# A hand-written order of work: w_out loaded in two halves around batch 1's k and v, half out-projection sums as filler, and a new order in every stage

## The chip, the cores and the metric

The kernel runs on one core of one Trainium2 chip. The metric is the device time of one execution in microseconds. The kernel before took 298.38 us in the median of 13 runs, from 297.27 to 302.06.

## The reference

Efficient attention (a softmax of q over the head dimension, a softmax of k over the sequence) feeds a gated feed-forward block. 8 batches, 8 heads, 576 positions, head dimension 64; the 4608 tokens of 512 features go through w_gate and w_val (512 x 1536) and w_out (1536 x 512).

```python
def _attn_ref(q, k, v):
    q_s = np.exp(q - np.max(q, axis=-1, keepdims=True))
    q_s = q_s / (np.sum(q_s, axis=-1, keepdims=True) + 1e-09)
    k_s = np.exp(k - np.max(k, axis=2, keepdims=True))
    k_s = k_s / (np.sum(k_s, axis=2, keepdims=True) + 1e-09)
    kv = np.einsum('bhsd,bhse->bhde', k_s, v)
    return np.einsum('bhsd,bhde->bhse', q_s, kv)

def _moe_ref(x, w_gate, w_val, w_out):
    g = x @ w_gate
    silu = g * (1.0 / (1.0 + np.exp(-g)))
    return (silu * (x @ w_val) @ w_out)

x = attn_out.transpose(0, 2, 1, 3).reshape(B * S, H * D)
```

## The kernel before

**Attention, per batch b and group G of four heads.** `exp` (L124) makes eq and ek from the loaded q and k on ScalarE. `cast_v` (L133) makes the bf16 v with a column of ones. `norm_sum` (L140) and `norm_mul` (L149) divide eq by its row sums to give qs. qs is transposed either by TensorE (`tr`, L158) or by a transposing DMA (`tr_dma`, L177, tile qtd). `kv` (L186) multiplies ek by v; `kn_recip` and `kn` (L200, L206) normalise it. `x` (L229) or `x_pair` (L260) multiply kn by the transposed q and cast the result into xt, the transposed input of the feed-forward block.

**Feed-forward.** Batch 0's tokens are taken whole: step I (`First`, L300) is a gate product with its Silu, step J the value product with its multiplication into hr, twelve of each. All other tokens are taken in chunks of 448 or 512 by `Pair` (L359): a pair of 128-column blocks of w_gate and w_val in seven products instead of eight, with sums of weights (gt, by `g_sum`, L333, steps Q and T) and sums of inputs (xs0 to xs3, by `x_sum`, L342, steps X for the next chunk and Y for this one). The steps of a pair are a, b, c, d, e, f, g on TensorE, with a copy, an addition or a Silu behind each, and v, an addition and a Silu. The block that is left over is done by `Direct` (L434), steps G and U.

**Out-projection.** Batch 0 goes by `Unit` (L470): step O is a token block and a half, so `O01` is the sum over the first six blocks of hr and w_out for token block 0, and `O02` the rest, with the copy and store. Later tokens go by `Quad` (L510), again seven products instead of eight, steps A, B, C, D, E, F, H, with sums of hr (hs, `h_sum`, L494, steps S) and sums of w_out (wt, `w_sum`, L488, steps W).

**The order.** Nothing is scheduled by a tool: each plan is a string of step names, and `chunk` (L746) issues them in that order, so every engine runs its own share of the steps in the order of the string. `PLAN_B` handles batch 0's I, J and O steps beside batch 1's attention, `PLAN_0` the rest of the first 1024 tokens, `PLAN` the five middle chunks, `PLAN_N` the two chunks after the last attention, `PLAN_E` the last out-projection. A number behind a colon is a batch; without one it is two ahead of the chunk. A star changes the engine:

```python
ceng = nc.vector if alt else nc.scalar        # copies of a Pair or Quad
meng = nc.vector if alt else nc.gpsimd        # multiplications into hr
elif nm == "cv":
    cast_v(b, G, nc.vector if alt else nc.gpsimd)
elif nm == "nd":
    norm_mul(b, G, nc.gpsimd if alt else nc.vector)
```

`si` and `pe` are tiny activations that load ScalarE's Silu or Exp table early. `kk` is kv with kn for batch 1, `xz` is x for batch 1, `lo` the loads of the next batch.

**Queues.** Loads of q, k and v, transposing DMAs and stores are issued from SyncE's queue (SP), in the order of the program; w_gate, w_val and w_out from GpSimd's queue (POOL), ahead of or between GpSimd's own work. `load` takes an `after`: the issue waits for that DMA to land. q has three buffers, k and v two each. PSUM has eight banks of one tag, shared by all steps.

Of the kernel before, what the change touches and what calls it, by code (L numbers as in the profile page):

```python
# [16 lines left out]
def kernel(  # L17
# [21 lines left out]
    B, H, S, D = q.shape  # L39
# [27 lines left out]
    wo = const.tile([128, MT, d_model], FP16, name="wo", tag="wo")  # L67
# [9 lines left out]
    dmas = {}  # L77
    raw = {}

    def load(b, G, what, src, after=None):  # L80
        raw[what, b, G] = ld.tile(
            [128, 2, T * 64], FP32, tag=what, name=what, bufs=3 if what == "q" else None
        )
        ap = bass.AP(
            tensor=src.tensor,
            offset=src[b, 4 * G].offset,
            ap=[[T * 64, 128], [2 * HSTR, 2], [1, T * 64]],
        )
        d = nc.sync.dma_start(out=raw[what, b, G], in_=ap)
        if after is not None:  # L90
            tc.add_manual_dep(d.ins, after.ins.name, SYNC, reason="order of loads")
        dmas[what, b, G] = d

    def load_group(b, G):
        for what, src in (("q", q), ("k", k), ("v", v)):
            load(b, G, what, src)
# [9 lines left out]
    def wo_slice(m0, n):  # L106
        ap = bass.AP(
            tensor=moe_w_out.tensor,
            offset=moe_w_out[m0 * 128, 0].offset,
            ap=[[d_model, 128], [128 * d_model, n], [1, d_model]],  # L110
        )
        return nc.gpsimd.dma_start(out=wo[:, m0:m0 + n, :], in_=ap)
# [9 lines left out]
    A, Z = BANKS = ((0, 5), (5, 9))  # L122
# [10 lines left out]
    def cast_v(b, G, eng, t0=0, t1=T):  # L133
        copy(
            eng,
            vbs[G][:, t0:t1, 0:128].rearrange("p t (h d) -> p t h d", d=64),
            raw["v", b, G].rearrange("p h (t d) -> p t h d", d=64)[:, t0:t1],
        )
# [38 lines left out]
    def tr_dma(b, G):  # L177
        s = st[b, G]
        qt = at.tile([128, T, 2, 64], BF16, tag="qtd", name="qtd")
        nc.sync.dma_start_transpose(  # L180
            out=qt.rearrange("p t g c -> p t (g c)"),
            in_=s["qs"].rearrange("p t c -> p (t c)"),
        )
        s["qt"] = [qt[:, :, g, :] for g in range(2)]
# [417 lines left out]
    with tc.manual_schedule():  # L602
# [22 lines left out]
        w_dma = []  # L625
# [6 lines left out]
        tc.add_manual_dep(w_dma[0].ins, dmas["k", 0, 0].ins.name, SYNC, reason="order of loads")  # L632
        load(1, 0, "q", q, after=w_dma[4])
        load(1, 1, "q", q)
        for m0 in (0, 4, 8):
            w_dma.append(wo_slice(m0, 4))
        tc.add_manual_dep(w_dma[7].ins, w_dma[5].ins.name, SYNC, reason="order of loads")

        warm_up(WARM[0])
# [18 lines left out]
        x(0, 1, A)  # L658
        x(0, 1, Z)

        load(1, 0, "k", k, after=w_dma[8])
        load(1, 0, "v", v)
        load(1, 1, "k", k, after=w_dma[9])
        load(1, 1, "v", v)
        load(2, 0, "q", q, after=dmas["k", 1, 0])
        load(2, 0, "k", k, after=dmas["v", 1, 0])
        load(2, 0, "v", v, after=dmas["k", 1, 1])
        load(2, 1, "q", q, after=dmas["v", 1, 1])
        load(2, 1, "k", k, after=dmas["q", 2, 0])

        n_ch = n_tok // 512 - 1

        def op(t, ci, c0, h, parts):
            alt = t.endswith("*")
            t = t.rstrip("*")
            t, b = t.split(":") if ":" in t else (t, ci + 2)
            b = int(b)
            k, a, nm = t[0], t[1:], t[:2]
            if nm in ATT:
                G = int(t[2]) if t[2:3].isdigit() else 0  # L680
                if b >= B or nm == "lo" and b + 1 >= B and ci >= 0:
                    return
                if nm == "eq":
                    exp(b, G, "q")
                elif nm == "ek":
                    exp(b, G, "k")
                elif nm in ("si", "pe"):
                    f = AF.Silu if nm == "si" else AF.Exp
                    nc.scalar.activation(out=warm, in_=zero[:, 0:1], func=f)
                elif nm == "cv":  # L690
                    cast_v(b, G, nc.vector if alt else nc.gpsimd)
                elif nm == "ns":
                    norm_sum(b, G)
                elif nm == "nm":
                    norm_mul(b, G, nc.vector if alt else nc.gpsimd)
                    tr_dma(b, G)
                elif nm == "lo":
                    if ci < 0:
                        load(b, 1, "v", v)
                    else:  # L700
                        load_group(b + 1, 0)
                        load_group(b + 1, 1)
                elif nm == "kv":
                    kv_pair(b)
                elif nm == "xx":
                    x_pair(b, nc.scalar if alt else nc.vector)
                elif nm == "nd":
                    norm_mul(b, G, nc.gpsimd if alt else nc.vector)
                elif nm == "tr":
                    tr(1, G, BANKS[int(t[3])], nc.vector)  # L710
                elif nm == "kk":
                    kv_kn(b, G, split=True)
                elif nm == "xz":
                    x(1, G, BANKS[int(t[3])], nc.scalar if alt else nc.vector)
            elif k in "abcdefgv":
                parts["p" + a].run(k, alt)
            elif k in "GU":
                parts["m" + a].run(k)
            elif k in "IJ":
                parts["i" + a].run(k)  # L720
            elif k == "O":
                parts["u" + a[0]].run(int(a[1]), alt)
            elif k in "ABCDEFH":
                parts["o"].run(k, alt)
            elif k in "SR":
                k0 = int(a[1])
                h_sum(ci + (k == "R"), int(a[0]), k0, k0 + int(a[2]))
            elif k == "X":
                if ci + 1 < n_ch:
                    x_sum(c0 + 2 * h, 256, int(a), nc.gpsimd if alt else nc.vector)  # L730
            elif k == "Y":
                x_sum(c0, h, int(a), nc.gpsimd if alt else nc.vector)
            elif k == "W":
                w_sum(int(a), nc.gpsimd if alt else nc.vector)
            elif k == "Q":
                g_sum(int(a), nc.vector if alt else nc.gpsimd)
            elif k == "T" and ci == B - 2:
                i = int(a)
                if i == 0:
                    parts["t"] = ld.tile(  # L740
                        [128, 4, 2, 2, 128 * (HM - NP)], FP16, tag="q", name="gt2", bufs=3
                    )
                gt2[i] = parts["t"][:, i]
                g_sum(i, nc.gpsimd if alt else nc.vector, 128 * NP, 128 * HM, gt2)
# [11 lines left out]
            for t in plan.split():  # L756
                op(t, ci, c0, n // 2, parts)

        ATT = ("pe", "eq", "ek", "si", "cv", "ns", "nm", "lo", "kv", "xx", "nd", "tr", "kk", "xz")
        ORDER = (0, 1, 2, 3, 4, 5)  # L760
        gt2 = [None] * 4
        PLAN_B = """
        I0 I1 pe:1 I2 I3 J0 J1 I4 I5 J2 J3 J4 Q0 I6 J5 I7 J6 J7 eq0:1 ns0:1 eq1:1 I8
        nd0:1* ns1:1 J8 I9 J9 I10 Q1* nd1:1* I11 cv0:1 tr00 J10 J11 tr10 ek0:1 O01 Q3*
        cv1:1 ek1:1 O11 tr01 kk0:1 O02 tr11 eq0:2 O12 kk1:1 ns0:2 O21 xz10* ek0:2 xz00*
        O22 Q2 xz01 eq1:2 cv0:2 xz11 O31 load:2 nm0:2 cv1:2 O32 ek1:2
"""
        PLAN_0 = """
        a0 ns1 G5 b0 G11 Y0 c0 Y2 Y1 v0 Y3* d0* W2 a1 f0 b1 U5 c1 g0 d1 W0 v1 e0 a2 f1 b2
        v2 kv silu:2 nm1 g1 d2 a3 e1 c2 f2 b3 c3 e2 g2 d3 v3 e3 a4 f3 xx* load g3 W1 d4*  # L770
        b4 c4* X0 f4 v4 U11 e4* X2* X1 W3 X3 g4*
"""
        PLAN = """
        a0 S042 b0 G5 c0 d0 A v0 S002 a1 f0 b1 S142 c1 v1 U5 S242 g0 pe S222 B S022 S102
        S122 S302 d1 S322 ek0 e0 a2 S342 e1 eq0 ns0 S202 C ek1 f1 D E eq1 cv1 b2 c2* silu
        F nm0 cv0 g1 d2 v2 ns1 a3 nm1 H* f2 kv g2 d3 b3 c3 v3 e2 load f3 e3 a4 b4 c4 g3 v4
        d4* e4 xx* f4 X2 G11 g4 X0 X1 X3* U11
"""
        PLAN_N = """
        a0 S222 b0 c0 d0 T0* A v0 S002 f0 a1 e0* S042 b1 g0 d1 c1 S022 v1 a2 f1 S242 S102  # L780
        b2 e1* c2 g1 S142 d2 v2 B f2 a3 T1* b3 c3 S342 S122 S202 g2* e2 d3 C S302 v3 f3
        e3* S322 a4 b4 g3* d4 c4 v4 D T2 f4 e4* a5 b5 g4* c5* X0* d5 F f5 v5 E T3* X1 e5*
        X3 g5* H* X2*
"""
        PLAN_E = """
        S022 A S042 S122 S002 S142 S202 B C S102 S302 S322 S242 S222 S342 D E F H*
"""
        chunk(-1, 0, S, PLAN_B)
        chunk(0, S, 1024 - S, PLAN_0)
        for ci in range(1, n_ch):  # L790
            chunk(ci, 512 * (ci + 1), 512, PLAN if ci + 2 < B else PLAN_N)
# [31 lines left out]
```

The softmax here doesn't subtract the row's maximum and nothing guards it: scores larger than these inputs give would overflow.

## Time and profile before

| | |
|---|---|
| Median of 13 runs | 298.38 us (297.27 to 302.06) |
| The profiled execution's own time | 297.96 us, span 296.1 us |
| TensorE (PE) busy | 286.2 us, 2716 matmuls |
| VectorE (DVE) busy | 240.9 us |
| ScalarE (ACT) busy | 221.4 us |
| GpSimd (POOL) busy | 156.1 us |
| TensorE clock granted | 1.00 throughout |
| Read from HBM, written | 37.75 MB, 9.44 MB |

| Stage, us from the span's start | length | PE busy | DVE | ACT | POOL |
|---|---|---|---|---|---|
| 15.70 to 36.30, batch 0's I and J steps | 20.60 | 19.91 | 10.20 | 15.45 | 7.85 |
| 36.30 to 55.90, rest of PLAN_B | 19.60 | 18.30 | 16.28 | 11.89 | 13.33 |
| 55.90 to 76.30, PLAN_0 | 20.40 | 19.09 | 16.92 | 15.90 | 14.71 |
| 106.30 to 136.25, a middle chunk | 29.95 | 29.95 | 26.40 | 25.34 | 19.27 |
| 253.70 to 281.20, a late chunk | 27.50 | 27.50 | 22.69 | 19.00 | 3.99 |

Times in the views are in microseconds from the first instruction unless they are marked ns. A row of the timeline gives the start, the length, the engine, the line and operation, the tiles and shapes and how many instructions were merged; square brackets hold the idle time ahead of it and what ended it. A row of the waits gives who waited for whom, the total, how often and the longest. A row of the groups gives the busy total and the mean of one in ns, then the idle time before. The matmuls of PE are pipelined, so that a record is longer (0.27 for 256 columns) than the interval from one start to the next (0.109).

### The profile page before, as it was taken

What the parts mean: (1) busy time and instruction counts of PE and PEld (TensorE: products, weight loads), DVE (VectorE), ACT (ScalarE), POOL (GpSimd) and SP (SyncE); (2) the same over time, 40 slices, a digit from 0 to 9 for tenths busy, and PEclk for the clock granted to TensorE, in tenths of its full rate; (3) what the DMA queues carried; (4) which work ended last, traced back from release to release, by engine and by line L of the source; (5) the groups of instructions that cost most, each with busy time, mean ns of one, the idle gap of its engine ahead of it and who ended that gap; (6) DMA issues with size and microseconds to landing.
All of it is one profiled execution on the core that took longest, in us unless ns stands there. A gap on an engine that the chain in (4) does not pass through costs nothing.

```text
span 296.1 us, 7118 instructions
## 1 busy us (share of the span) xinstructions
PE 286.2 (97%) x2716; PEld 233.8 (79%) x2716; DVE 240.9 (81%) x490; ACT 221.4 (75%) x416; POOL 156.1 (53%) x128
## 2 busy tenths in 40 slices
PE   8999998998999999999999999999999999999992
PEld 6877664587888878887888688868887888888882
DVE  2935696797999889988898889888999898897881
ACT  5684955877799689968996889688969775778431
POOL 1903856679329852975197619761977444031000
PEclk9999999999999999999999999999999999999999
DMA  7999999928903793199326961795192000500065
GB/s 261 292 192 245 243 320 380 269 62 161 359 2 72 151 355 129 23 188 348 147 51 138 295 224 39 152 321 193 30 152 45 0 2 1 125 19 2 9 136 143
DMA packets 38338, 46.47 MB, mean 157 GB/s; under 512 B 16288, under 2 KB 21408, under 8 KB 38304
## 3 DMA queue, kind: packets, MB, share of 16 engines
q1 hardware_dynamic: 32864, 41.03, 48.4%
q0 software_dynamic: 5280, 4.72, 10.0%
q8 instruction: 21, 0.34, 0.5%
q10 hardware_dynamic: 160, 0.26, 0.2%
q14 instruction: 13, 0.11, 0.1%
HBM read 37.75 MB, written 9.44 MB: 159 GB/s over the span
## 4 chain that ended last, share of the span: by engine, by line
PE 74%; DMA 15%; POOL 3%; ACT 3%; DVE 2%; issue 1%; ACTq 0%; SPq 0%; DVEq 0%; POOLq 0%
PE sx L388 23%; PE ox L533 13%; PE sw L388 11%; PE ow L533 7%; PE sy L388 6%; DMA wg<-in_moe_w_gate_dram 4%; DMA q<-in_q_dram 4%; PE oy L533 4%; DMA wo<-in_moe_w_out_dram 3%; PE u_ps L441 3%; PE g_ps L441 3%; PE kv L192 2%; DMA qtd<-qs 2%; POOL qs L152 1%; PE o_ps L479 1%; DMA k<-in_k_dram 1%
## 5 line engine op out<-in xcount | busy, mean ns | idle before, releaser
L388 PEld LDWEIGHTS <-gt 128*128 128x128 f16 x672 | 64.6, 98 | 13.5 <-issue 3.0
L432 POOL TENSOR_TENSOR hr<-sg,u 128x512 bf16<-128x512 f16 (+1 forms) x33 | 39.1, 1184 | 51.5 <-ACT sg L431 50.5
L388 PE MATMUL sx<-xs,gt 128*128 128x256 f16 (+1 forms) x336 | 49.9, 271 | 0.3 <-DVE s L118 0.3
L116 ACT COPY s<-sx 128x512 f32<-128x512 f32 (+1 forms) x77 | 44.3, 577 | 7.7 <-PE sx L388 7.4
L423 POOL TENSOR_TENSOR hr<-sg,u 128x512 bf16<-128x512 f16 (+1 forms) x31 | 36.5, 1185 | 23.1 <-DVE u L422 22.3
L533 PEld LDWEIGHTS <-hs 128*128 128x128 bf16 x384 | 37.2, 98 | 4.7
L152 POOL TENSOR_TENSOR qs<-eq,rr 128x1152 bf16<-128x1152 bf16 x15 | 32.6, 2179 | 9.2 <-DVE rr L147 6.0
L388 PEld LDWEIGHTS <-wg 128*128 128x128 f16 x336 | 32.8, 98 | 4.8
L427 DVE TENSOR_TENSOR u<-sx,s 128x512 f16<-128x512 f32 (+1 forms) x42 | 28.5, 679 | 9.8 <-ACT sg L414 4.0
L414 ACT ACTIVATE sg<-s 128x512 f16<-128x512 f32 (+1 forms) x42 | 26.2, 625 | 12.8 <-DVE s L412 11.0
L431 ACT ACTIVATE sg<-sx 128x512 f16<-128x512 f32 (+1 forms) x42 | 25.2, 601 | 10.7 <-PE sx L388 10.6
L533 PEld LDWEIGHTS <-hr 128*128 128x128 bf16 x288 | 28.2, 98 | 3.3
L412 DVE TENSOR_TENSOR s<-sy,s 128x512 f32<-128x512 f32 (+1 forms) x42 | 28.3, 675 | 2.7 <-PE sy L388 2.1
L422 DVE TENSOR_TENSOR u<-sw,s 128x512 f16<-128x512 f32 (+1 forms) x42 | 28.4, 675 | 2.5 <-PE sw L388 1.2
L143 DVE TENSOR_REDUCE rs<-eq 128x18 f32<-128x1152 bf16 x16 | 21.4, 1340 | 7.0 <-ACT eq L127 7.0
L388 PE MATMUL sx<-xt,gt 128*128 128x256 f16 (+1 forms) x168 | 25.0, 271 | 0.0
L388 PE MATMUL sw<-xs,wv 128*128 128x256 f16 (+1 forms) x168 | 25.0, 271 | 0.0
L388 PE MATMUL sy<-xt,wg 128*128 128x256 f16 (+1 forms) x168 | 25.0, 271 | 0.0
L388 PE MATMUL sw<-xs,gt 128*128 128x256 f16 (+1 forms) x168 | 24.9, 271 | 0.0
L388 PE MATMUL sx<-xt,wg 128*128 128x256 f16 (+1 forms) x168 | 24.9, 271 | 0.0
L116 ACT COPY s<-sw 128x512 f32<-128x512 f32 (+1 forms) x34 | 19.8, 582 | 5.4 <-PE sw L388 5.2
L533 PE MATMUL ox<-wt,hs 128*128 128x256 f16 x192 | 23.6, 273 | 0.0
(101 smaller groups left out, 552.4 us busy)
## 6 DMA issues: line engine op xcount, KB each, us to landing
q<-in_q_dram SPq DMA_DIRECT2D x16, 576.0 KB, 6.5
k<-in_k_dram SPq DMA_DIRECT2D x16, 576.0 KB, 6.5
v<-in_v_dram SPq DMA_DIRECT2D x16, 576.0 KB, 7.1
out_dram<-o_sb SPq DMA_DIRECT2D x70, 128.0 KB, 2.4
wv<-in_moe_w_val_dram POOLq DMA_DIRECT2D x3, 512.0 KB, 11.2
wo<-in_moe_w_out_dram POOLq DMA_DIRECT2D x3, 512.0 KB, 10.1
wg<-in_moe_w_gate_dram POOLq DMA_DIRECT2D x2, 512.0 KB, 11.2
wg<-in_moe_w_gate_dram POOLq DMA_DIRECT2D x2, 256.0 KB, 5.0
```

The source lines that it names most:

```text
L116: nc.scalar.copy(out=out, in_=in_)
L143: nc.vector.reduce_sum(out=rs, in_=s["eq"].rearrange("p t h d -> p (t h) d"), axis=mybir.AxisListType.X)
L152: eng.tensor_mul(s["qs"].rearrange("p t (h d) -> p (t h) d", d=64), s["eq"].rearrange("p t h d -> p (t h) d"), s["rr"].to_broadcast([128, ...
L388: nc.tensor.matmul(out=bank[:, h * j:h * j + h], lhsT=wgt(kk, j), rhs=rhs[:, kk, 0:h], start=first and j == 0 and kk == 0, stop=kk == 1, s ...
L412: nc.vector.tensor_add(self.s1, self.y[:, 0:w], self.s1)
L414: nc.scalar.activation(out=self.sa[:, 0:w], in_=self.s1, func=AF.Silu)
L422: nc.vector.tensor_add(u, self.w[:, 0:w], self.s2)
L423: meng.tensor_mul(self.out(0), self.halves(self.sa), self.halves(u))
L427: nc.vector.tensor_add(self.u, self.x[:, 0:w], self.s5)
L431: nc.scalar.activation(out=sb[:, 0:w], in_=self.x[:, 0:w], func=AF.Silu)
L432: meng.tensor_mul(self.out(1), self.halves(sb), self.halves(self.u))
L533: nc.tensor.matmul(out=dst[p][:, 0:HN], lhsT=lhs(kk, p), rhs=rhs(kk), start=start and i == 0, stop=i == HM - 1, skip_group_check=True,)
```

## The change

w_out is loaded in four slices of three blocks instead of three slices of four. The first two stand where the slices stood. The other two (`wo`) are issued from the plan, on GpSimd's queue, after J11. Batch 1's k and v of group 0 no longer wait for w_out but for batch 1's q; k of group 1 waits for the second slice. The load of v for batch 2's group 1 has a step of its own (`lv`). PLAN_B is merged into PLAN_0, in a new order with other engines for some steps, and the other plans have new orders too, with the stars placed anew.

```diff
--- before.py
+++ after.py
@@ -632,8 +632,8 @@
         tc.add_manual_dep(w_dma[0].ins, dmas["k", 0, 0].ins.name, SYNC, reason="order of loads")
         load(1, 0, "q", q, after=w_dma[4])
         load(1, 1, "q", q)
-        for m0 in (0, 4, 8):
-            w_dma.append(wo_slice(m0, 4))
+        for m0 in (0, 3):
+            w_dma.append(wo_slice(m0, 3))
         tc.add_manual_dep(w_dma[7].ins, w_dma[5].ins.name, SYNC, reason="order of loads")
 
         warm_up(WARM[0])
@@ -658,15 +658,15 @@
         x(0, 1, A)
         x(0, 1, Z)
 
-        load(1, 0, "k", k, after=w_dma[8])
+        load(1, 0, "k", k, after=dmas["q", 1, 1])
         load(1, 0, "v", v)
-        load(1, 1, "k", k, after=w_dma[9])
-        load(1, 1, "v", v)
-        load(2, 0, "q", q, after=dmas["k", 1, 0])
-        load(2, 0, "k", k, after=dmas["v", 1, 0])
-        load(2, 0, "v", v, after=dmas["k", 1, 1])
-        load(2, 1, "q", q, after=dmas["v", 1, 1])
-        load(2, 1, "k", k, after=dmas["q", 2, 0])
+        load(1, 1, "k", k, after=w_dma[8])
+        load(1, 1, "v", v, after=dmas["k", 1, 0])
+        load(2, 0, "q", q, after=dmas["k", 1, 1])
+        load(2, 0, "k", k, after=dmas["v", 1, 1])
+        load(2, 0, "v", v, after=dmas["q", 2, 0])
+        load(2, 1, "q", q, after=dmas["k", 2, 0])
+        load(2, 1, "k", k, after=dmas["v", 2, 0])
 
         n_ch = n_tok // 512 - 1
 
@@ -678,7 +678,7 @@
             k, a, nm = t[0], t[1:], t[:2]
             if nm in ATT:
                 G = int(t[2]) if t[2:3].isdigit() else 0
-                if b >= B or nm == "lo" and b + 1 >= B and ci >= 0:
+                if b >= B or nm == "lo" and b + 1 >= B:
                     return
                 if nm == "eq":
                     exp(b, G, "q")
@@ -694,12 +694,14 @@
                 elif nm == "nm":
                     norm_mul(b, G, nc.vector if alt else nc.gpsimd)
                     tr_dma(b, G)
+                elif nm == "lv":
+                    load(2, 1, "v", v)
+                elif nm == "wo":
+                    wo_slice(6, 3)
+                    wo_slice(9, 3)
                 elif nm == "lo":
-                    if ci < 0:
-                        load(b, 1, "v", v)
-                    else:
-                        load_group(b + 1, 0)
-                        load_group(b + 1, 1)
+                    load_group(b + 1, 0)
+                    load_group(b + 1, 1)
                 elif nm == "kv":
                     kv_pair(b)
                 elif nm == "xx":
@@ -756,36 +758,33 @@
             for t in plan.split():
                 op(t, ci, c0, n // 2, parts)
 
-        ATT = ("pe", "eq", "ek", "si", "cv", "ns", "nm", "lo", "kv", "xx", "nd", "tr", "kk", "xz")
+        ATT = ("pe", "eq", "ek", "si", "cv", "ns", "nm", "lo", "kv", "xx", "nd", "tr", "kk", "xz", "lv", "wo")
         ORDER = (0, 1, 2, 3, 4, 5)
         gt2 = [None] * 4
-        PLAN_B = """
-        I0 I1 pe:1 I2 I3 J0 J1 I4 I5 J2 J3 J4 Q0 I6 J5 I7 J6 J7 eq0:1 ns0:1 eq1:1 I8
-        nd0:1* ns1:1 J8 I9 J9 I10 Q1* nd1:1* I11 cv0:1 tr00 J10 J11 tr10 ek0:1 O01 Q3*
-        cv1:1 ek1:1 O11 tr01 kk0:1 O02 tr11 eq0:2 O12 kk1:1 ns0:2 O21 xz10* ek0:2 xz00*
-        O22 Q2 xz01 eq1:2 cv0:2 xz11 O31 load:2 nm0:2 cv1:2 O32 ek1:2
-"""
         PLAN_0 = """
-        a0 ns1 G5 b0 G11 Y0 c0 Y2 Y1 v0 Y3* d0* W2 a1 f0 b1 U5 c1 g0 d1 W0 v1 e0 a2 f1 b2
-        v2 kv silu:2 nm1 g1 d2 a3 e1 c2 f2 b3 c3 e2 g2 d3 v3 e3 a4 f3 xx* load g3 W1 d4*
-        b4 c4* X0 f4 v4 U11 e4* X2* X1 W3 X3 g4*
+        I0 I1 I2 I3 J0 J1 J2 I4 I5 J3 I6 J4 I7 I8 J5 pe:1 J6 eq0:1 J7 J8 eq1:1 I9 I10
+        ns0:1 ns1:1 J9 I11 Q2 J10 ek0:1 nd1:1 nd0:1* O01 tr00 tr01 tr10 tr11 cv0:1 kk0:1
+        ek1:1 Q0* O11 cv1:1* xz00* xz01* O21 kk1:1 J11 wo xz10* Q1 eq0:2 lv xz11 O31 a0 b0
+        Y0* ek0:2 O02 ns0:2 c0 O12 W0 Y1 Y2 cv1:2 d0 nm0:2 O22 Y3 eq1:2 ek1:2 Q3* W1 f0 v0
+        a1* b1 cv0:2 e0 g0 G5 d1* c1 ns1:2 v1 nm1:2 a2 f1 O32 kv:2 g1 d2 b2 c2 v2 e1 f2 a3
+        G11 e2* b3 g2 v3 U5 d3* xx:2* load:2 c3* f3 W2* a4* silu:2 b4 c4 g3 v4 d4* U11 X0*
+        f4 e3* e4* X2 X1 W3 g4* X3
 """
         PLAN = """
-        a0 S042 b0 G5 c0 d0 A v0 S002 a1 f0 b1 S142 c1 v1 U5 S242 g0 pe S222 B S022 S102
-        S122 S302 d1 S322 ek0 e0 a2 S342 e1 eq0 ns0 S202 C ek1 f1 D E eq1 cv1 b2 c2* silu
-        F nm0 cv0 g1 d2 v2 ns1 a3 nm1 H* f2 kv g2 d3 b3 c3 v3 e2 load f3 e3 a4 b4 c4 g3 v4
-        d4* e4 xx* f4 X2 G11 g4 X0 X1 X3* U11
+        S002 pe a0 b0 c0 A d0 S042 S242 S142 S022 B eq0 S102 eq1 S122 G5 v0 f0 e0 S202 a1
+        b1 D v1 c1* S222 S322 g0* S302 a2* d1 C S342 e1 cv0 cv1 f1 ek0 F E ek1 g1 d2 b2 H*
+        c2 ns1 v2 a3 nm1 ns0 f2 b3 nm0 kv g2 d3 c3 v3 a4 f3 b4 e2* e3 c4 g3 d4 v4 e4 G11
+        f4 xx X2 load X0 X1 U5 X3 g4* silu U11
 """
         PLAN_N = """
-        a0 S222 b0 c0 d0 T0* A v0 S002 f0 a1 e0* S042 b1 g0 d1 c1 S022 v1 a2 f1 S242 S102
-        b2 e1* c2 g1 S142 d2 v2 B f2 a3 T1* b3 c3 S342 S122 S202 g2* e2 d3 C S302 v3 f3
-        e3* S322 a4 b4 g3* d4 c4 v4 D T2 f4 e4* a5 b5 g4* c5* X0* d5 F f5 v5 E T3* X1 e5*
-        X3 g5* H* X2*
+        S002 a0 b0 c0 d0 A v0 S042 S022 f0 B a1 S142 S102 g0* b1 d1 c1 S242 v1 a2 S222
+        S122 e0 f1 b2 S202 S302 D g1 d2 c2 v2 e1* a3 f2 S322 e2 b3 c3 g2 v3 d3* C f3 T0 a4
+        b4 v4 T1* e3* g3 T2* d4 S342 c4 F f4 a5 b5 T3* g4 d5* e4 c5 v5 f5 E e5* g5* X0 X1
+        H* X2 X3
 """
         PLAN_E = """
-        S022 A S042 S122 S002 S142 S202 B C S102 S302 S322 S242 S222 S342 D E F H*
+        S022 S042 S002 S142 S122 S342 A S102 S242 S222 S202 S322 B S302 C D* E F H*
 """
-        chunk(-1, 0, S, PLAN_B)
         chunk(0, S, 1024 - S, PLAN_0)
         for ci in range(1, n_ch):
             chunk(ci, 512 * (ci + 1), 512, PLAN if ci + 2 < B else PLAN_N)
```

## The prediction

> **What bounds the kernel now.** I read the page's busy shares first. PE is busy 97%, but the Trainium skill (Perfetto Trace Analysis, section Identifying the Most-Contended Engine) warns that matmul busy time of a pipelined engine says little of headroom, so I checked it against the work. In the chain of waits the kv matmuls of the middle chunks start at 96.28, 126.25, 156.22, 186.18 and 216.15, a period of 29.97. The matmuls of a chunk, at the start-to-start intervals in the trace, are 224 of 256 columns x 0.109 = 24.4, 16 of 512 x 0.216 = 3.5, kv 1.2 and the x matmuls 0.85: 29.9. So the middle is full, and nothing can be won there. Next the waits of PE, with the rows of its timeline:
>
> ```profile
> PE 286.2 (97%) x2716; PEld 233.8 (79%) x2716; DVE 240.9 (81%) x490; ACT 221.4 (75%) x416; POOL 156.1 (53%) x128
> ```
> ```profile
> PE kv L192 <- POOL vb L118: 1.1, 2, 0.7
> PE xa L273 <- DMA qtd<-qs: 0.9, 1, 0.9
> PE g_ps L310 <- ACT sg L321: 0.7, 1, 0.7
> ```
> ```profile
> 36.33 2.26 PE L310 MATMUL g_ps<-xt,wg 128*128 128x320 f16 x16 [0.72 <-ACT sg L321]
> ...
> 44.65 0.70 PE L192 MATMUL kv<-vb,ek 64*128 64x129 bf16 x18 [0.73 <-POOL vb L118]
> ...
> 48.62 0.70 PE L192 MATMUL kv<-vb,ek 64*128 64x129 bf16 x18 [0.35 <-POOL vb L118]
> ...
> 51.16 0.46 PE L237 MATMUL xp<-qt,kn 64*64 64x320 bf16 x6 [0.19 <-ACT kn L212]
> ...
> 59.82 0.54 PE L388 MATMUL sx<-xs,gt 128*128 128x224 f16 x4 [0.33 <-DVE s L118]
> ...
> 72.45 0.33 PE L273 MATMUL xa<-qtd,kn 64*64 64x320 bf16 x4 [0.94 <-DMA qtd<-qs]
> ```
> All avoidable waits lie between 35 and 76 us. Counted from start to start, less the nominal interval (a wait costs a drained pipeline too), they are 0.89, 0.89, 0.51, 0.51, 0.50 and 1.21, with two small ones 0.20 and 0.17: **4.9 us**, the most that a new order can win before the tail. Why kv is late stands in the chain:
>
> ```profile
> 27.31 10.12 DMA wo<-in_moe_w_out_dram
> ...
> 37.48 4.01 DMA k<-in_k_dram
> ...
> 41.50 7.30 DMA q<-in_q_dram
> ```
> Batch 1's k leaves only when the second third of w_out has landed (37.42), so exp, the cast of v and kv follow the transfer.
>
> **What the skill says.** GPSIMD Engine Reference, Specifications: GpSimd shares its SBUF interfaces with VectorE, and they contend when a VectorE instruction has two SBUF inputs. The trace agrees: an h_sum of VectorE (L502) takes 0.416 alone and up to 1.36 when a GpSimd run is under way; gt at 37.91 took 2.78 and ended 0.69 after GpSimd's qs, where its twin took 0.81. It works both ways: the cast of v at 60.19 took 1.45 instead of 1.14. DMA: Bandwidth & Descriptors, Queues, rings and completion order: a DMA engine round-robins between queues by packet. The trace agrees: q of batch 1 (SP queue) and the last w_val slice (POOL queue) finish together, at 30.8 and 30.5.
>
> **The change, part by part.** The orders on each engine come from building both kernels, the durations from the profile. PE has the same 2716 matmuls.
>
> *Batch 0, 15.7 to 38.4.* 23 I and J steps of 0.98 from 15.72 end at 38.4. exp(q) of batch 1 ends when q lands (33.35) + 1.2 = 34.55, plus a table load 1.28 and Silu 0.75 frees I9's banks at 36.6. Before, I10 came 20 steps in (35.4) and waited for Silu behind those exps; now the first step that wants these banks is J10 at 37.4. The 0.89 goes.
>
> *DMAs.* Two w_out slices of three blocks are 1.5 x 2.55 = 3.8 instead of 2 x 2.55 us of transfer ahead of k(1,1); k(1,0) and v(1,0) leave at 33.4 instead of 37.5. With 1.5 a load, k(1,0) lands at about 37.3 (was 41.5), v(1,0) 38.9 (43.3), k(1,1) 40.3, v(1,1) 41.8 (47.3). The other two slices are issued on GpSimd behind the cast of v(1,0), at about 40 (2 x 0.76, hidden: the next GpSimd work waits for VectorE's gt at 44). They share the engines with q and k of batch 2. Each later load waits for the one two ahead, so v(2,1) lands at about 55, between 52.4 (3.5 from issue to landing, nothing in its way) and 57.
>
> *38.4 to 55.* O01 (1.29) and tr00, tr01 end at 40.2. tr10 needs qs of group 1, now on VectorE: it is free at 39.3, but the cast of v(1,0) holds the port to 40.05, and the multiply needs 1.2: 41.2, **a stall of 0.9** (0.3 to 1.3). exp(k) is done at 40.8: kv runs at once. Then out-projection halves fill. The next kv waits for the cast of v(1,1), moved to VectorE behind gt (2 x 0.8) from 43.3: about 1.3 for 1152 elements (640 took 0.77), to 46.1; PE is there at 45.5: **0.6**. x of group 1 waits for J11's multiply in one bank: **0.4**. The wo halves land long before O02 at 50.8.
>
> *55 to 75.* VectorE runs seven two-input sums in a row (W0, Y1 to Y3, two gt, W1), 51.3 to 55.8; f0's addition comes behind them and g0 wants it at 57.1. GpSimd then waits for v(2,1): cast, qs (2.1), cast, to 60.4, just ahead of kv at 60.8. Small waits there and at g1: **0.4**. The second qtd leaves GpSimd at about 64.7 and takes 4.5 as at 67.74: 69.2 against x at 68.8: **0.4** (was 1.21). End: 0.1. Sum 2.8 against 4.9: **2.1 won**. I take 0.5 off for a landing of v(2,1) inside that run (below).
>
> *Middle chunks.* VectorE takes three multiplies (0.425), three casts of x (1.6) and X3 (0.42): +3.3; it loses port waits, (0.62-0.42) and (0.59-0.42) x 3 in L502 and L506 and 0.5 in X2: -1.6. 26.4 + 1.7 = 28.1 of 29.95. GpSimd loses 4.7. ScalarE loses 1.5 of casts, but exp is split in two places with Silu between: two more table loads of 1.28; 25.4 + 1.0 = 26.4. Walking a chunk from a0, the deadlines that come nearest: d0 (2.6) needs a0's copy behind a table load (2.2); f2 (18.3) needs d2's copy behind g1's reload (17.5 to 18.2); g2 (20.4) needs f2's addition (20.1); the second qtd lands at 25.5 to 26.3, x at 27. All hold, none by much. I take **0.1 lost in all**, 0 to 0.3 a chunk as bounds. c0 of chunk 1 waits for X0 on GpSimd, behind W2 (about 3.1, scaled from 2.61 for 1280 columns): ready at 75.1, wanted at 75.8.
>
> *Last chunks and tail.* Seven multiplies and two copies of VectorE instead of eight and one, A later in VectorE's order but at the same place on PE: no change. The tail after the last matmul keeps its order: 0.
>
> Sum: 297.96 (the profiled execution: span 296.1 and 1.9 around it) - 2.1 + 0.5 + 0.1 = 296.5; that execution lies 0.4 under the median 298.38, so **296.8**.
>
> **Rivals.**
> (1) *The gain is given back in the start-up, no change.* The casts and qs on GpSimd come later than I walk (v(1,0) after 39.4, v(2,1) after 57): tr10, kv(2) and qtd lose 1 to 2 us more. For it: the loads' landings are estimates. Against: they are issued 4 us earlier. About 298.3.
> (2) *GpSimd takes the port inside VectorE's run, slower.* If v(2,1) lands before about 53.3, GpSimd's cast, qs and cast (1.15 + 2.1 + 1.15) can slip between the seven sums, since a waiting engine seems to be served when an instruction ends (the h_sum at 90.54 got in between two GpSimd runs). The last sum ends 60, g0 waits 3.6 instead of 0, later waits of 0.8 vanish: net 2.8 more lost, 299.6. For it: the lower bound 52.4. Against: the w_out slices in the way.
> (3) *ScalarE becomes the bound in the middle, slower.* If the reloads make copies late by 0.5 in five chunks: 2.5, 299.3. For it: margins of 0.1 to 0.4. Against: back-to-back ScalarE records overlap by 0.1 each, which I did not credit.
> (4) *Everything holds*, including the port: up to 4 won, 294.6.
>
> **How the numbers follow.** Forecast 0.48 (own range 295.6 to 297.4), rival 4 0.06, rival 1 0.2, rivals 2 and 3 0.13 each. 0.3% of 298.4 is 0.9 us, about what a measurement of this kernel can tell from no change. Faster: forecast and rival 4, less a little of the forecast's upper end, 0.52; same 0.21; slower 0.27. Range 295.0 to 299.8: outside lie most of rival 4 and the bad ends of 2 and 3.
>
> **What would show it.** Right: no wait of g_ps for sg near 35; kv of batch 1 at about 41.8 (was 44.65); a wait of tp or kv of some 0.9 near 40.5 and one of kv for VectorE's cast near 45.5; the first sx of chunk 1 near 75 (was 76.48); the kv period still 29.97. Wrong: g0 waiting over 2 us near 57 behind the sums (rival 2), a period over 30.2 (rival 3), or kv of batch 1 at 44 (rival 1).

## The result: slower, and the profile after

The changed kernel takes **302.91 us** in the median of 11 runs, from 301.72 to 309.01, against 298.38 us: a ratio of **1.0139** (95% interval 1.0117 to 1.0161), some 4.2 us more. Ratios, here and below, leave out executions that lie over 1.5% above the fastest of their kernel (10 of 22 in the run e11); medians do not. The profiled execution took 302.49 us, with a span of 300.3.

First the page's busy shares after the change:

```profile
PE 288.0 (96%) x2716; PEld 235.3 (78%) x2716; DVE 243.0 (81%) x530; ACT 221.9 (74%) x401; POOL 135.4 (45%) x112
```

As many matmuls, in a span 4.2 us longer, with 1.8 us more of busy time: matmuls must have become slower somewhere too. The waits of PE (total, times, longest) and the rows of its timeline that answer to those of before:

```profile
PE kv L192 <- POOL vb L118: 3.2, 2, 2.9
PE kv L192 <- DVE vb L118: 2.2, 1, 2.2
```
```profile
41.25 0.70 PE L192 MATMUL kv<-vb,ek 64*128 64x129 bf16 x18 [0.32 <-POOL vb L118]
...
47.31 0.70 PE L192 MATMUL kv<-vb,ek 64*128 64x129 bf16 x18 [2.19 <-DVE vb L118]
...
65.28 1.22 PE L192 MATMUL kv<-vb,ek 64*128 64x129 bf16 x36 [2.92 <-POOL vb L118]
66.44 0.92 PE L388 MATMUL sx<-xt,gt 128*128 128x224 f16 x4
67.15 0.95 PE L388 MATMUL sx<-xs,gt 128*128 128x224 f16 x4
...
70.03 0.55 PE L388 MATMUL sx<-xs,gt 128*128 128x224 f16 x4
```

kv of batch 1 starts 3.4 us earlier than before (44.65), and no g_ps waits for sg near 35 any more. But kv now stands still twice for a cast of v. And behind the second pause a row of four matmuls of 224 columns takes 0.95 instead of 0.55. The windows (PE, PEld, DVE, ACT and POOL busy, then the granted clock, the DMA share and GB/s) give that stretch a number:

```profile
62.00:66.00 4.00, 1.08 (x28) 0.81 (x27) 1.14 (x3) 3.02 (x7) 4.00 (x4) 1.00 0.14 28
66.00:70.00 4.00, 4.00 (x38) 3.27 (x33) 2.15 (x9) 1.44 (x3) 4.00 (x4) 0.57 0.56 111
```

The chain of waits (start, length) has lost the w_out transfer that stood in it before. It now goes from batch 1's v over the casts and gt:

```profile
33.20 6.07 DMA v<-in_v_dram
...
39.40 1.80 POOL vb L118
...
42.56 1.56 DVE gt L340 x2
44.12 3.15 DVE vb L118
47.27 0.04 issue
47.31 0.70 PE kv L192 x18
...
64.14 1.10 POOL vb L118
65.24 0.04 issue
65.28 0.74 PE kv L192 x19
```

Who makes the casts late stands in the timelines of VectorE and GpSimd:

```profile
42.56 1.56 DVE L340 TENSOR_TENSOR gt<-wv,wg 128x1280 f16<-128x1280 f16 x2
44.03 3.22 DVE L118 CAST vb<-v 128x1152 bf16<-128x1152 f32 x1
```
```profile
43.47 6.11 POOL L340 TENSOR_TENSOR gt<-wv,gt 128x1280 f16<-128x1280 f16 x2 [0.76 <-DVE gt L340]
...
60.92 1.14 POOL L118 CAST vb<-v 128x1152 bf16<-128x1152 f32 x1 [8.78 <-DMA v<-in_v_dram]
62.03 2.12 POOL L152 TENSOR_TENSOR qs<-eq,rr 128x1152 bf16<-128x1152 bf16 x1
64.09 1.14 POOL L118 CAST vb<-v 128x1152 bf16<-128x1152 f32 x1
```

VectorE's cast of v(1,1) takes 3.22 us and ends 0.7 after GpSimd's first gt sum (the row of 6.11 holds two, the first from 43.47 to 46.57). GpSimd stands idle for 8.78 us until v(2,1) has landed at 60.8, and the cast of v(2,0), whose data had been there since 52.8, comes only behind that cast and a multiply: kv starts at 65.28.

Start-to-start, by stage:

| | before | after | difference |
|---|---|---|---|
| to the first I step | 15.72 | 15.28 | -0.44 |
| from there to the first sx of chunk 1 | 60.76 | 64.83 | +4.07 |
| chunks 1 to 7 | 204.98 | 205.92 | +0.94 |
| last out-projection to its last matmul's end | 9.36 | 9.41 | +0.05 |
| from there to the end | 5.29 | 4.85 | -0.44 |

The 0.94 is 0.26 and 0.24 in chunks 1 and 3, 0.23 and 0.28 in the two late chunks; the other middle chunks are within 0.03 of 29.97.

### The profile page after: what moved, and what is told of

The parts are those of the page before. It is cut to its first block, busy times and chain, and to the rows that moved or that the text cites. A ratio compares the mean times of both kernels' runs of the same rounds, so it can differ in the third digit from the quotient of the medians.

```text
span 300.3 us, 7094 instructions
## 1 busy us (share of the span) xinstructions
PE 288.0 (96%) x2716; PEld 235.3 (78%) x2716; DVE 243.0 (81%) x530; ACT 221.9 (74%) x401; POOL 135.4 (45%) x112
## 4 chain that ended last, share of the span: by engine, by line
PE 82%; DMA 7%; DVE 4%; POOL 3%; ACT 1%; issue 1%; ACTq 0%; SPq 0%; DVEq 0%; POOLq 0%
PE sx L388 23%; PE ox L533 12%; PE sw L388 11%; PE ow L533 7%; PE sy L388 6%; PE warm_ps L256 4%; PE u_ps L441 4%; PE oy L533 3%; PE g_ps L441 3%; PE kv L192 3%; DMA q<-in_q_dram 3%; DMA v<-in_v_dram 2%; PE g_ps L310 2%; POOL qs L152 2%; PE o_ps L479 2%; DMA qtd<-qs 2%
## 5 line engine op out<-in xcount | busy, mean ns | idle before, releaser
L423 POOL TENSOR_TENSOR hr<-sg,u 128x512 bf16<-128x512 f16 (+1 forms) x28 | 32.1, 1147 | 100.2 <-DVE u L422 47.1
L388 PEld LDWEIGHTS <-gt 128*128 128x128 f16 x672 | 65.5, 98 | 14.2 <-issue 1.5
L116 ACT COPY s<-sx 128x512 f32<-128x512 f32 (+1 forms) x70 | 40.7, 582 | 8.3 <-PE sx L388 8.0
L431 ACT ACTIVATE sg<-sx 128x512 f16<-128x512 f32 (+1 forms) x42 | 24.7, 589 | 16.7 <-PE sx L388 11.5
L432 POOL TENSOR_TENSOR hr<-sg,u 128x512 bf16<-128x512 f16 (+1 forms) x27 | 30.7, 1138 | 14.0 <-ACT sg L431 14.0
L152 POOL TENSOR_TENSOR qs<-eq,rr 128x1152 bf16<-128x1152 bf16 x14 | 29.5, 2120 | 6.0 <-DVE rr L147 6.0
L116 ACT COPY s<-sw 128x512 f32<-128x512 f32 (+1 forms) x36 | 21.4, 594 | 9.6 <-PE sw L388 9.6
L388 PE MATMUL sw<-xs,wv 128*128 128x256 f16 (+1 forms) x168 | 24.2, 273 | 0.0
```

Source lines behind the costliest of these rows:

```text
L116: nc.scalar.copy(out=out, in_=in_)
L152: eng.tensor_mul(s["qs"].rearrange("p t (h d) -> p (t h) d", d=64), s["eq"].rearrange("p t h d -> p (t h) d"), s["rr"].to_broadcast([128, ...
L388: nc.tensor.matmul(out=bank[:, h * j:h * j + h], lhsT=wgt(kk, j), rhs=rhs[:, kk, 0:h], start=first and j == 0 and kk == 0, stop=kk == 1, s ...
L423: meng.tensor_mul(self.out(0), self.halves(self.sa), self.halves(u))
L431: nc.scalar.activation(out=sb[:, 0:w], in_=self.x[:, 0:w], func=AF.Silu)
L432: meng.tensor_mul(self.out(1), self.halves(sb), self.halves(self.u))
```

## Experiments

**One cast at a time.** Theory T: the two late casts and the slow stretch behind the second are the loss; R1: the later orders are; R2: the held cast is most of it.

```diff
- Q0* O11 cv1:1* xz00* xz01* O21 kk1:1 J11 wo xz10*      # e1
+ Q0* O11 wo cv1:1 xz00* xz01* O21 kk1:1 J11 xz10*
- a1* b1 cv0:2 e0                                        # e2; e4 has both
+ a1* b1 cv0:2* e0
```

> The cast of v(1,1) goes from VectorE back to GpSimd, ahead of its gt sum; the two w_out slices are issued ahead of it, so that they leave as before. Theory T (two late casts of v, the second set by the landing of v(2,1) at 60.8 and by GpSimd's order behind it, then a slow stretch of TensorE): the cast ends at about 44.8, kv(1,1) at 45 does not wait and the 2.2 us there are gone, but TensorE now reaches kv of batch 2 at about 60.0 instead of 62.3, and the cast it waits for still ends near 65.2: its wait grows from 2.9 to some 5.2, and the total stays at 302.5 to 302.9. Rival R2 (VectorE's held cast is the main loss by itself): the gain of 2.3 stays, 300.6. Rival R1 (the loss lies in the new orders of the later chunks): no change, and no growth of the wait at kv of batch 2.

Measured 302.81 us, ratio 1.014 (1.0078 to 1.0201): no change, as T has it. But the 2.2 us went elsewhere than expected. The waits of PE:

```profile
PE o_ps L479 <- DMA wo<-in_moe_w_out_dram: 2.5, 1, 2.5
PE kv L192 <- POOL vb L118: 2.4, 2, 2.1
```

TensorE, 2 us earlier, runs into the fourth w_out slice (landed at 53.7); kv of batch 2 still starts at 65.56, when v(2,1)'s cast and what stands behind it are done. R2's 300.6 lies just outside the wide interval of these four executions, and e4 below repeats the finding with 18. R2 falls: the held cast is hidden by transfers that come later.

> The cast of v(2,0) goes from GpSimd, where it stands behind the cast of v(2,1) and a 2.1 us multiply, to VectorE at the same place of the order. T: VectorE does it near 59.5 to 61 in about 1.3 us, GpSimd being idle there; v(2,1)'s cast ends at 62.1 as before, TensorE comes to kv of batch 2 at 62.3 and does not wait; without the pause TensorE's matmuls behind it run at full rate: 3.1 + 1.65 = 4.7 us less, 298.2. If the slow stretch is not due to the pause, 299.8. R1 (later orders): at most 1 us less, 302. If GpSimd's multiply holds VectorE's cast (3 us instead of 1.3): 299.5 to 300.

Measured 300.92 us, 1.0071 (1.0047 to 1.0094): 2.0 us won, not 4.7. In the profiled execution the slow stretch is gone (clock 1.000). VectorE's timeline gives the cast without GpSimd beside it:

```profile
59.34 0.81 DVE L118 CAST vb<-v 128x1152 bf16<-128x1152 f32 x1
```

0.81 us, where the same cast took 3.22. What took the place of the stall, in PE's timeline:

```profile
64.46 1.20 PE L192 MATMUL kv<-vb,ek 64*128 64x129 bf16 x35 [1.20 <-ACT sg L431]
...
73.72 0.33 PE L273 MATMUL xa<-qtd,kn 64*64 64x320 bf16 x4 [1.48 <-ACT xt L116]
```

ScalarE's exp of k(2,1) waits until that load lands at 60.84; the table load and the Silus stand behind it in order, and kv's second bank waits for one of them.

> Both edits: v(1,1) cast on GpSimd, v(2,0) cast on VectorE. T: TensorE reaches kv of batch 2 at about 60.0, v(2,1) still lands near 60.8 and its cast ends at 62.1: a wait of about 2.1, which only replaces the one removed at 45; total as with v(2,0)'s cast moved alone, 298.0 (299.6 if a pause of 2.1 us is enough for a slow stretch). R2: the gains add, 295.8.

Measured 300.87 us, 1.0079 (1.0055 to 1.0103): as e2 alone, so the gains do not add. R2 is out again. T has the size of the wait (2.1), but neither its last releaser, since kv now waits 1.88 for ScalarE, behind k(2,1), nor the time of 298.0.

**Where the landing comes from.** In the kernel before, each load waits for one four loads ahead (q(2,0) for k(1,0), k(2,1) for q(2,0)); in the changed one mostly for one two ahead. T2: with two loads under way the engines run dry. R3: w_out beside the loads lowers the rate. Rows of SyncE's queue in the changed kernel (q, k, v of group 0, then of group 1):

```profile
40.77 0.37 SPq L89 DMA_DIRECT2D q<-in_q_dram  x1
43.62 0.37 SPq L89 DMA_DIRECT2D k<-in_k_dram  x1
47.02 0.37 SPq L89 DMA_DIRECT2D v<-in_v_dram  x1
51.52 0.37 SPq L89 DMA_DIRECT2D q<-in_q_dram  x1
52.83 0.37 SPq L89 DMA_DIRECT2D k<-in_k_dram  x1
53.24 0.47 SPq L89 DMA_DIRECT2D v<-in_v_dram  x1
```

Between 47.4 and 51.5 nothing is issued: the queue waits for k(2,0) to land (51.51).

```diff
- load(2, 0, "v", v, after=dmas["q", 2, 0])
- load(2, 1, "q", q, after=dmas["k", 2, 0])
- load(2, 1, "k", k, after=dmas["v", 2, 0])
+ load(2, 0, "v", v)
+ load(2, 1, "q", q, after=dmas["q", 2, 0])
+ load(2, 1, "k", k)
```

With both cast edits:

> Both cast edits, and three waits between loads loosened: v(2,0) is issued without a wait, q(2,1) waits for q(2,0) instead of k(2,0), k(2,1) for nothing. Order of instructions unchanged. Theory T2 (what is left is the landing of k(2,1) and v(2,1), late because SyncE's queue stands still until k(2,0) has landed, and ScalarE's exp of k(2,1) holds the Silus behind it): q, k and v of group 1 leave near 46 instead of 52.5, v(2,1) lands near 58.5 instead of 61 to 63, ScalarE is free of exp at 60.2, kv of batch 2 waits 0.3 instead of 2.1, x of batch 2 does not wait (1.5 before): 3.2 us less than with both casts alone, 297.6. Rival R3 (the transfers themselves are the limit, w_out and the loads of batch 2 share the engines at a lower rate): v(2,1) lands where it did, within 1 us: 300.5 to 301.

Measured 299.07 us, 1.0025 (0.9997 to 1.0054). v(2,1) landed at 58.0, as T2 has it; R3's 300.5 lies outside. The profiled execution took 297.98 us, 0.4 above T2's 297.6: VectorE's cast met GpSimd again, and PE waited 1.0 for the copy behind it. The median is 1.1 higher still, which this profile does not explain. VectorE's row, then GpSimd's:

```profile
58.35 1.64 DVE L118 CAST vb<-v 128x1152 bf16<-128x1152 f32 x1
```
```profile
59.27 2.57 POOL L152 TENSOR_TENSOR qs<-eq,rr 128x1152 bf16<-128x1152 bf16 x1
```

Then the loads alone, in the changed kernel:

> The changed kernel with the three waits between loads loosened and nothing else; both casts stay where the change put them. T2 (v(2,1) lands late because SyncE's queue stands still until k(2,0) has landed; GpSimd's order and the slow stretch follow from that): v(2,1) lands near 58, GpSimd's cast, multiply and cast end at 62.4, TensorE is at kv of batch 2 at 62.3: a wait of 0.1 to 0.3 instead of 2.9, no slow stretch there, 4.5 us less: 298.3. The 2.2 us for VectorE's cast at 45 stay. R3 (rate of transfer): 302 to 302.9.

Measured 299.49 us, 1.0032 (1.0011 to 1.0052): 3.4 us won by three waits, short of the 4.5 expected. In the profiled execution (300.81 us, 1.3 above the median) v(2,1) landed at 59.3, issued at 50.0, since q(2,0) landed late there; kv of batch 2 did not wait, but the slow stretch had come behind the first pause, and x of batch 2 waited 1.3 for the second qtd. One window of the kernel before, two of the changed kernel, then two of the kernel with casts and loads:

```profile
46.00:50.00 4.00, 3.65 (x36) 1.96 (x35) 1.85 (x9) 2.52 (x4) 2.58 (x2) 1.00 1.06 391
```
```profile
50.00:54.00 4.00, 4.00 (x26) 2.42 (x25) 3.90 (x9) 3.05 (x5) 1.03 (x1) 1.00 0.70 199
...
58.00:62.00 4.00, 4.00 (x34) 2.92 (x31) 3.58 (x7) 3.12 (x4) 1.07 (x1) 1.00 0.46 167
```
```profile
50.00:54.00 4.00, 3.57 (x25) 2.14 (x23) 3.90 (x7) 2.20 (x4) 2.29 (x2) 1.00 1.05 403
...
58.00:62.00 4.00, 2.98 (x25) 2.21 (x24) 4.00 (x5) 3.97 (x6) 3.83 (x3) 1.00 0.03 11
```

The DMA share is 1.06 in the kernel before. From 50 to 54 it is 0.70 in the changed kernel and 1.05 in the one with casts and loads, which is done with them at 58.

**The title's edit undone, and its loads alone.**

```diff
- for m0 in (0, 3):                                      # e12, with `wo` out of the plan
+ for m0 in (0, 3, 6, 9):
```

> The title's edit undone in the changed kernel: all four w_out slices are issued where the three stood, none from the plan. T2 and R3 both: batch 1's k and v share the engines with w_out and land about 2 us later, kv of batch 1 at 43 instead of 41.25. R3 (the two late slices slow the loads of batch 2): those now run undisturbed, v(2,1) lands by 56.5 although the waits stay, no wait at kv of batch 2: 299 to 300. T2 (the waits alone): v(2,1) still lands after 59 and the pause ahead of kv of batch 2 stays at 2 or more: 302 to 304.

Measured 302.53 us, 1.0137 (1.0097 to 1.0177): no better. With w_out out of the way the loads of batch 2 are still issued one by one, v(2,1) lands at 63.3 and DMA share is 0.69 from 46 to 50. R3's forecast (56.5, 299 to 300) falls, and with it rate as the only cause. But k and v of batch 1 land 3 to 5 us later here, so the loads of batch 2 also start later, and kv of batch 1 waits 3.0. Counted from the issue of q(2,0) to the landing of v(2,1), the loads take 20.0 us in the changed kernel (40.77 to 60.80), 17.4 without w_out beside them (e12), 18.0 with the waits loosened (e10) and 16.7 with waits and casts (e8). So sharing the engines with w_out has a part in the late landing too. How large it is with batch 1's loads on time was not tested.

The other way round, the loads alone in the kernel before, with its plans:

```diff
- for m0 in (0, 4, 8):                                   # e9, with the changed kernel's waits
+ for m0 in (0, 3):
- Q3* cv1:1 ek1:1 O11
+ Q3* wo cv1:1 ek1:1 O11
```

> One part of the change alone: the kernel before, with its plans, but w_out in four slices of three, two of them issued on GpSimd ahead of the cast of v(1,1), and the waits between the loads of the changed kernel. T2: kv of batch 1 no longer waits (0.9 and 0.5 us), but v(2,1) lands at 62 instead of 60.0, with kv of batch 2 wanted at some 62.5: 1.0 to 1.5 us less, 297.2. R3: the w_out slices slow k and v of group 1 and of batch 2, v(2,1) lands after 63: 298.5 to 299.5. If the split were itself the loss: 302.

Measured 305.78 us, 1.0235 (1.0172 to 1.0297), far above every expectation. I had not asked when the old plan first uses the second half of w_out. PE's waits:

```profile
PE o_ps L479 <- DMA wo<-in_moe_w_out_dram: 6.7, 2, 4.4
```

O02 stands right behind batch 1's first kv there, which ends at 44.7; the two late slices land at 49.1 and 52.5. A split load needs work in between that does not read the second half, as the new order has it with its half sums. Half rate adds to the loss: behind these pauses the clock is 0.50 from 49.48 to 56.30.

**The later orders.** The kernel before up to chunk 0, with the new plans behind it:

```diff
- PLAN = "a0 S042 b0 G5 ..."                             # e6, and so PLAN_N and PLAN_E
+ PLAN = "S002 pe a0 b0 c0 ..."
```

> The other part alone: the kernel before up to and with chunk 0, then the new plans of the middle, late and last chunks. From the start of chunk 1 on the changed kernel lost 0.26 + 0.24 + 0.23 + 0.28 us in four chunks and won 0.45 behind its last matmul. T and T2: 0.3 to 0.6 more than before, 298.9. R1 (the new later orders are the loss): 301 or more.

Measured 299.42 us, 1.0023 (1.0006 to 1.0039): 0.7 us more than before. R1 as the main cause falls; as a small part it stands.

**The slow stretch.** Extra matmuls on zeros, into the bank that kv overwrites next:

```diff
+ if (b, G) == (2, 0):                                   # e7; e14: also (1, 1), with 20
+     for _ in range(26):
+         nc.tensor.matmul(out=s["kv"][0][:, 0:256], lhsT=zero[:, 0:128], rhs=zero, start=True, stop=True)
```

> The changed kernel with 26 extra matmuls of 256 columns on zeros (2.8 us of TensorE) put into the pause ahead of kv of batch 2, into the bank that kv then overwrites; nothing else differs. T: kv starts at 65.3 as before, but TensorE has not been idle, and the 20-odd matmuls behind it take 0.096 instead of 0.187: 1.65 us less, 301.3. If the slow stretch comes from something else (data, memory, other engines), 302.9.

Measured 302.05 us, 1.0108 (1.0076 to 1.0141). In its profile the matmuls behind kv of batch 2 run at full rate, but now those from 49 to 52 do not, behind the pause of 2.19 at 47.7. So both were filled:

> The changed kernel with extra matmuls on zeros in both pauses: 20 (2.2 us) ahead of kv of batch 1's group 1, 26 (2.8 us) ahead of kv of batch 2, each into the bank that this kv overwrites. The waits for the casts stay. Theory C (a pause of 2 to 3 us makes TensorE run at half rate for the next 3.4 us, after which pause being a matter of phase): the granted clock is 1.000 instead of 0.991, and 1.6 us go: 301.3. If the slow stretch has another cause it is still there, 302.9.

Measured 301.70 us, 1.0093 (1.0066 to 1.0120). The mean clock is 0.996 to 1.000 in all 14 executions, against a median of 0.990 in the changed kernel. Theory C holds: the stretch comes from the pauses. By the two ratios it was worth about 1.4 us, with the waits themselves left in place, though their intervals just overlap.

Which pause it follows can be read from the traces. In all 14 profiles each stretch of full clock lasts a whole multiple of 3.413 us: 18 of them in the changed kernel (5.04 to 66.48), 13 in e7 (4.70 to 49.08). Four such windows of the changed kernel (length, PE busy, clock, DMA share, GB/s), then two of e7:

```profile
42.59:46.00 3.41, 2.53 (x18) 1.00 1.06 251
46.00:49.41 3.41, 2.10 (x31) 1.00 1.15 256
...
63.07:66.48 3.41, 1.20 (x37) 1.00 0.33 62
66.48:69.89 3.41, 3.41 (x21) 0.50 0.49 101
```
```profile
45.66:49.07 3.41, 1.37 (x24) 1.00 1.11 212
49.08:52.49 3.41, 3.34 (x17) 0.50 1.04 313
```

In the changed kernel the pause of 2.19 is split between two windows, which keep 2.53 and 2.10 us of busy time, and nothing follows; the pause of 2.92 leaves 1.20 in its last window, and the next one runs at half rate. In e7 the same 2.19 lies almost whole in one window, leaves 1.37, and the next is slow. Between 25 and 82 us of the 14 profiles, all seven windows with 2.03 us or more of idle time were followed by half rate, and none of those with 1.84 or less.

**A version to beat both.** Both cast edits, with VectorE's cast right behind W1, the loosened loads and the old `PLAN` and `PLAN_N`:

```diff
- Q3* W1 f0 v0 a1* b1 cv0:2 e0                           # e11, with e1's and e8's edits
+ Q3* W1 cv0:2* f0 v0 a1* b1 e0
- PLAN = "S002 pe a0 b0 c0 ..."
+ PLAN = "a0 S042 b0 G5 ..."
```

> A version meant to beat both: the loosened loads, v(1,1) cast on GpSimd, v(2,0) cast on VectorE right behind its run of sums (while GpSimd waits for v(2,1)), the old plans of the middle and late chunks, the new plan of the last. With both casts and loads alone the profiled span was 295.9. T2: the 1.0 us wait for VectorE's copy at 61 goes (the cast no longer meets GpSimd's multiply), the 0.20 + 0.23 + 0.28 of chunks 1, 6 and 7 go: span 294.2, time 296.3 where no slow stretch comes. Rival (something else is late next, VectorE's additions behind the cast or the second transposed q): 297.9, no better than both casts and loads.

Median 300.14 us, 1.7 above that of the kernel before in the same series, with a ratio of 1.0003 (0.998 to 1.0026): no better than before. The rival had it: the wait at 61 is gone, and two others stand in its place, as PE's waits show.

```profile
PE o_ps L479 <- DMA wo<-in_moe_w_out_dram: 1.4, 1, 1.4
...
PE xa L273 <- DMA qtd<-qs: 1.0, 1, 1.0
```

The same with these two pauses filled:

```diff
- Y0* ek0:2 O02 ns0:2 c0                                 # e13
+ Y0* ek0:2 fw O02 ns0:2 c0                # fw: 14 matmuls on zeros into c0's bank
+ if (b, G) == (2, 1):                     # in x_pair, ahead of group 1
+     fill(ps[1][0], 11)
```

> The version meant to beat both (casts moved, loads loosened, old later plans) with 14 extra matmuls in the pause ahead of O02, where it waits 1.4 us for w_out, and 11 in the pause of 1.0 us ahead of x of batch 2, into banks that are overwritten next. Theory C: pauses this short also cost rate in many executions, the fillers prevent it, and the mean granted clock stays over 0.995: 298.2 in the median, ratio to before 0.999. If the clock loss has another cause: 300, with a clock of 0.990 in half of the executions.

Measured 299.10 us, 1.0015 (0.9985 to 1.0045); the clock is 0.995 or more in all 14 executions, so the fillers do to the clock what C says, but the time is that of before, 0.9 above the 298.2 expected. No version tried is measurably faster than the kernel before.

## Why the prediction failed, step by step

*What held.* The forecast was 296.8 us, 302.91 was measured. J10 no longer waits for Silu: the 0.89 at 35 is gone. kv of batch 1 starts at 41.25 (forecast 41.8). Its neighbours came near in sum, in part by luck: tr10 and kv lose 0.51 + 0.48 start to start (forecast 0.9 for tr10 alone). VectorE's multiply was not held by GpSimd's cast, as forecast; it began first, at 38.84, and GpSimd's cast from 39.40 took 1.79 instead of 1.14, so that kv waited for it too. x of group 1 loses 0.45 + 0.23 (0.4). Rival 2 did not happen: VectorE's seven sums ran undisturbed from 52.56 to 56.69. Nor did rival 3: no copy of ScalarE was late by 0.5 in the middle.

*The step that failed most: "Each later load waits for the one two ahead, so v(2,1) lands at about 55", with bounds of 52.4 and 57.* It landed at 60.80. I had counted transfers at 1.5 us a load, as if the engines were always full, and read past what the quoted words say: two loads under way instead of four. The Trainium skill (SBUF — State Buffer, section The DMA setup-cost knee) puts a fixed part of about 2 us beside the transfer of every DMA, most of it the confirmation at the end. The trace agrees in kind: the first load of the program takes 3.6 us from issue to landing, against 1.5 from one landing to the next where the engines are full, and beside w_out it is more, 7.9 for k(2,0). Loosening the waits alone won 3.4 of the 4.5 us expected of it. So rival 1, "v(2,1) after 57", was the right mechanism, with 1 to 2 us where 3.1 and the slow stretch were due. What follows the landing was right: cast, multiply and cast took 4.3 us (forecast 4.4), and kv starts when they end.

*The cast of v(1,1): "about 1.3 for 1152 elements", a stall of 0.6.* The stall was 2.35 start to start. My rule was that GpSimd and VectorE contend when VectorE has two SBUF inputs; this cast has one. But the skill's line (GPSIMD Engine Reference, Specifications) names a 2-port mode too, and VectorE: DVE Perf Modes, section Mode 2×_2P, says that an operation with one source, such as a copy, can use both read ports where source and destination lie in SBUF. The measured 0.81 alone, 1.64 beside the end of a cast and a multiply, and 3.22 beside gt fit those sections; 1.3 was scaled from a shorter cast. Yet e1, and e4 against e2, show no gain from taking this cast off VectorE: what was due behind it was later still.

*The slow stretch* was in no step. The Trainium skill (TensorE: Matmul & The Clock Gate, Part 1) has it: half rate after at least one idle window of some 3.4 us, in windows that run on regardless of the kernel. The windows above agree on length and regularity, but not on "idle": 2.03 us without work in a window were enough. Here it cost about 1.4 to 1.6 us.

*The middle: "0.1 lost in all", the late chunks and tail 0.* Measured 0.43 in the middle, 0.51 in the late chunks and 0.44 won in the tail; their sum, 0.5, lies in e6's interval (0.2 to 1.2). Of the middle, 0.26 is x of chunk 3, which waits for its second qtd until 167.70, and 0.21 is d0 of chunk 1, at 82.94: two of the deadlines that the forecast had named as near.

*The sum.* The forecast's own terms add up to 296.9, not 296.8, which changes nothing. Stalls of 2.8 were forecast for the start-up; 7.1 came (0.51, 0.48, 2.35, 0.45, 0.23 and 3.08), and 1.6 of slow matmuls. Even with the loads mended, chunk 1 starts at 76.03 (e8) against 76.48: e1, e8 and e11 run into transfers that end at 58 and w_out slices that land at 52 to 54. These, and not only the 4.9 us of waits that I took as the budget, limit what an order can win here.

## What to carry over

When loads are chained by waits, count how many are under way at a time and set their time from issue to landing against it; here a chain two deep left the engines partly idle (DMA share 0.70 from 50 to 54) where one four deep had filled them (1.06 from 46 to 50 in the kernel before). Before a wait is counted as won, ask what is due next and when it can be there at the earliest: here three removed stalls in a row uncovered a later landing. A one-input cast in SBUF is not safe beside GpSimd (0.81 us alone, 3.22 beside a sum), and a stall of 2 us on TensorE can cost some 1.7 us more (half rate for 3.4), if it falls into one window of the clock.

## What the runs showed that I had not expected

A pause much shorter than the 3.4 us window is enough for half rate, and where it lies in the row of windows decides. The stretch came behind 2.92 us idle in the changed kernel and behind 2.19 in e7; the same 2.19 did nothing in the changed kernel, where it was split between two windows. The stretch lasts one window: a clock of 0.57 over 4 us is (1 - 0.57) x 4 / 0.5 = 3.4 us at half rate, a loss of 1.7. In e9, with two windows of long waits in a row, it lasted two.

A cast on VectorE (0.81 us alone) can take four times as long beside one GpSimd sum (3.22), while GpSimd's own sums only stretch from 2.60 to 3.10. GpSimd's cast of v can be the one that is held: 1.14 alone, 1.79 at 39.40 beside VectorE's multiply, which had begun first.
